# A seventh head pair's scores from fp32 operands, the last output tile's last product in column halves, and a new set of planner constants

## The chip, the cores and the metric

The kernel runs on one core of a Trainium2 chip. The metric is the device time of one execution in microseconds. A profiled execution has a time of its own and, inside it, a span from the first to the last instruction; positions in the trace are counted from the start of the span. All times below are microseconds unless marked ns.

## The reference

Attention with a causal mask over 4 batches of 12 heads, 448 positions, 64 columns a head, and then a block on the joined heads (768 channels):

```python
scores = scale * np.matmul(q, k.transpose(0, 1, 3, 2))
scores = np.where(mask, -1000000000.0, scores)
attn = np.exp(scores - max) / (sum + 1e-09)
x = (attn @ v), heads joined to (4, 448, 768)
theta = x @ w_theta
y = einsum(w_tok_r, x * cos(theta)) + einsum(w_tok_i, x * sin(theta))
u = x + y
out = u + np.maximum(u @ w_ch, 0.0)
```

Inputs and outputs are fp32; the weights arrive as fp64 and are brought to fp32 on the chip.

## The kernel before

**Numbers in two parts.** Most matmul operands are split into a rounded part and a remainder (both F32R tiles), and a product is made from two or three of the combinations. A product of two unsplit fp32 operands is written as one matmul, which the trace shows as two instructions.

**Attention.** Heads go in pairs, six pairs to a batch, 24 in all. `load_pair` brings a pair's q, k and v. A pair whose number is under `KN["NQ"]` (6) takes the fp32 way: k into one `kk` buffer (ring of 3) and each head's half of q into the two zero-padded `qz` tiles, slot `pr % 2`, three loads in all. Every later pair takes the split way: k and q into `kr` and `qr` (one buffer each), a rounding copy and a subtraction for each (L402, L403, recorded at L331 to L342), and then four stores from SBUF to SBUF for each head (L409, L411), which lay the two parts into `kk` and `qs`. `head` makes the four score blocks of a head, 448, 336, 224 and 112 columns wide: L441 by fp32, L444 by two F32R matmuls. VectorE masks and finds the minimum (L447), ScalarE makes the exponential and its sums (L450), TensorE transposes (L474), ScalarE or VectorE copies the result back (L334, L336). A pair's sums are turned into reciprocals (L457, L458), transposed (L459, in the one-bank PSUM ring `xo`), copied (L460), stored to DRAM (`rd<-rs`) and read back spread over the partitions (`rb<-rd`, one buffer). The product with v (L491) uses the same `xo` bank, which L494 frees as it multiplies it by `rb` into `xT`.

**The block on the heads.** `weight` decodes w_theta and w_tok; `batch` makes theta (L540), sine and cosine, and the mix over positions (L620). `project` makes the last product for batches 1 and 2 (L682). `pair` makes it for batches 3 and 0 together by seven smaller products of three 128-row output tiles each (L749). `block` prepares the three operand chunks `ub` of each such product: a rounding copy and a subtraction. `last` finishes an output tile: an addition of the bank to a partial sum (`add`, recorded at L757), a maximum with zero and an addition (L769), and the store. The last of the seven products (`s4`, with `end`) goes tile by tile, so that the last tile's nine matmuls stand alone at the end.

**The order.** No order is written out. Every operation gets a due time `P.now`, and `Plan.order` lays all of them out by a list schedule: at each moment a free engine takes the ready operation with the smallest due time, an engine that is not the first choice counting `AP` or `AQ` later. The resulting sequence is the program order of each engine and of the queue on SyncE (SP), which issues every DMA. The constants in `KN` set the due times: `S0`, `P0`, `P1` the pace of the heads (`tau`); `TL`, `RL`, `V`, `BB` the transposes, reciprocals and products with v; `LD`, `SL`, `SH` the loads and splits of q and k; `LW`, `W0`, `WT`, `W1`, `WK`, `E0`, `CR` the weights; `M0`, `MR`, `MR2`, `X0`, `XL`, `EX` a batch's block; `O0`, `OR` the last products; `UL`, `UD` the chunks `ub`, of which chunk c is due at the clock of the products less `UL` plus `UD` times c; `SB`, `SC` the combined weights. Up to due time `AE` GpSimd may take copies.

Of the kernel before, what the change touches and what calls it, by code (L numbers as in the profile page):

```python
# [13 lines left out]
ALU = mybir.AluOpType  # L14
# [4 lines left out]
MAGIC = 12582912.0  # L19


KN = dict(S0=-2520.8995, P0=3914.469, P1=7056.6972, V=0.0339, TL=0.8835, RL=-0.0438, SL=7631.8556, SH=2896.8187,
          LD=2238.5021, LW=-1908.5532, M0=-3353.0467, MR=1.7842, MR2=-0.0229, W0=15032.9046, WT=3030.4005,
          W1=2485.321, WK=2746.2629, E0=-8178.3792, CR=419.9564, O0=2180.1597, OR=0.4535, X0=-265.4206, NS=1, PR=2,
          AE=15377.7073, BB=-1728.1953, AP=5033.1175, AQ=2425.1203, XT=3, NQ=6, WP=2, NW=4, EX=0.4254, PORT=1,
          DW=1450, DE=150, DB=250.0, SL2=0, UL=1823.0792, UD=372.3266, SB=51637.6906, SC=462.9947, XL=-895.2931,
          TS=0.2508, SW=3360.6242, WQ=2)


class Buf:  # L30
# [11 lines left out]
class Plan:  # L42
# [12 lines left out]
    def op(self, eng, dur=None, fn=None, r=(), w=(), lat=None, pr=None, table=None, after=(), port=("POOL",), pen="AP", mode="m"):  # L55
        o = Op()
        o.pen = KN[pen]
        o.port = port
# [38 lines left out]
    def order(self):  # L97
# [53 lines left out]
        while done < len(self.ops):  # L151
# [10 lines left out]
            for e in free:  # L162
# [3 lines left out]
                for o in ready[e]:  # L166
                    if port > t and e in o.port and KN["PORT"]:
                        continue
                    if best is not None and (o.pr > best.pr + KN["SW"] or turn(last[0], o.mode)):
                        continue  # L170
# [23 lines left out]
                if o.wire:  # L194
                    wire = max(wire, fin + KN["DW"]) + o.wire
                    end = wire + KN["DE"]
                out.append((t, o.idx, o))
# [10 lines left out]
                for x in o.succ:  # L208
                    x.n -= 1
                    x.ready = max(x.ready, end + max(delay(e, a) for a in x.alts) + KN["SL2"])  # L210
                    if not x.n:
# [8 lines left out]
def attention_moe_kernel(  # L220
# [10 lines left out]
    nc = tc.nc  # L231
    B, NP, _, S = q.shape
# [27 lines left out]
    P = Plan(rings)  # L260
# [35 lines left out]
    def pe(n, m=128):  # L296
        return {112: 75, 224: 102.5, 336: 153, 384: 173.7, 448: 206.7}[n]

    def dv(n):
        return n / 0.96 + 68  # L300
# [13 lines left out]
    def dma(fns, nbytes, r=(), w=(), pr=None, after=(), half=False):  # L314
        def run():
            for f in fns():
                nc.sync.dma_start(out=f[0], in_=f[1])  # L317
        n = nbytes[0]
        o = P.op("SP", 530 if n == 1 else 615.0 * n, run, r, w, lat=0, pr=pr, after=after)
        o.wire = nbytes[1] / KN["DB"]  # L320
        return o
# [3 lines left out]
    def copy(n, o, i, r, w, psum=False, engs=("DVE", "ACT"), after=()):  # L325
        alts = []
        if not psum and P.now <= KN["AE"]:
            engs = tuple(engs) + ("POOL",)
# [10 lines left out]
    def alu(n, o, a, b, op, r, w, engs=("POOL", "DVE"), after=(), pool=False):  # L339
        if P.now > KN["AE"] and not pool:  # L340
            engs = ("DVE",)
# [6 lines left out]
    def boost(h):  # L348
        return KN["BB"] * max(0, h % H - (H - 3)) / 2
# [33 lines left out]
    def load_pair(pr):  # L383
        b, p = divmod(pr, NP)
        t0 = tau(2 * pr)
        if pr < KN["NQ"]:
            kp = buf("kk", [128, 2, S])
            dma(lambda: [(kp.t[:, 0], k[b, p])], (1, 229376), [], [kp], pr=t0 - KN["LD"] - 50000)
            for hh in range(2):
                own = slice(64 * hh, 64 * hh + 64)  # L390
                qz, i = QZ[hh], pr % 2
                dma(lambda qz=qz, own=own, i=i: [(qz.t[own, i], q[b, p, own])], (1, 114688), [], [(qz, i)],
                    pr=t0 - KN["LD"] + hh - 49999)
                KS[2 * pr + hh], QS[2 * pr + hh] = kp, (qz, i)
        else:
            t1 = t0 - KN["SL"]
            parts = []
            for n, (ring, src) in enumerate((("kr", k), ("qr", q))):
                y = buf(ring, [128, 2, S], F32R)
                dma(lambda y=y, src=src: [(y.t[:, 1].bitcast(F32), src[b, p])], (1, 229376), [], [(y, 0), (y, 1)], pr=t1 - KN["LD"])  # L400
                P.now = t1 + 300 * n
# [12 lines left out]
        vs = buf("vs", [TQ, NJ, 2, D])  # L414
        dma(lambda: [(vs.t, v[b, p])], (1, 229376), [], [vs], pr=t0 - KN["LD"] + 1000)
        VS[pr] = vs
# [6 lines left out]
    def head(h):  # L423
# [42 lines left out]
        for n, js in enumerate(((2,), (3, 1), (0,))):  # L466
            P.now = t0 + per * (KN["TL"] + (1.5, 3, 4)[n] * KN["TS"]) - boost(h)
            pt = buf("t", [TQ, S])
# [190 lines left out]
        return clock[0]  # L659

    NC = KD // 2


    def project(b, wb, t0, rate, after):
# [10 lines left out]
        for m in range(KD):  # L675
            cp = buf("st"[m % 2], [128, 512], F32, "cp")
            for p in range(KD):
                wt, wk = wb[2 * (m // NC) + p // NC]

                def mm(p=p, m=m, cp=cp, wt=wt):  # L680
                    for n, (w2, a) in enumerate(((0, 0), (0, 1), (1, 0))):
                        nc.tensor.matmul(out=cp.t[:, 0:S], lhsT=wt()[:, p % NC, w2, 128 * (m % NC):128 * (m % NC) + 128],  # L682
                                         rhs=us[p].t[:, a], start=(p == 0 and n == 0), stop=(p == KD - 1 and n == 2))
# [11 lines left out]
    def pair(ba, bb, xa, xb, t0, rate, wb, ws, after, end=False):  # L695
        clock = [t0]
        ka = lambda p: [(xa, (p, 0)), (xa, (p, 1))]
        kb = lambda p: [(xb, (p, 0)), (xb, (p, 1))]
        ua = lambda p: (lambda: xa.t[:, p])
        vb = lambda p: (lambda: xb.t[:, p])  # L700
        u2, u3 = buf("R", [128, NC, S], F32, "u2"), buf("R", [128, NC, S], F32, "u3")
        q1 = buf("xs", [128, NC, S], F32, "q1")

# [37 lines left out]
        def product(w, ub, banks, first, inner=True):  # L741
            wt, wk = w
            for x in range(NC):
                for y in range(NC):
                    m, c = (y, x) if inner else (x, y)

                    def mm(m=m, c=c):
                        for n, (w2, a) in enumerate(((0, 0), (0, 1), (1, 0))):
                            nc.tensor.matmul(out=banks[m].t[:, 0:S], lhsT=wt()[:, c, w2, 128 * m:128 * m + 128],  # L749
                                             rhs=ub[c].t[:, a], start=(first and c == 0 and n == 0),  # L750
                                             stop=(c == NC - 1 and n == 2), skip_group_check=True)
                    clock[0] += 3 * pe(S) * rate
                    P.now = clock[0]
                    P.op("PE", 3 * pe(S), mm, [(ub[c], 0), (ub[c], 1)] + wk(c), [banks[m]])

        def add(o, a, b, op, r, w):
            P.op("DVE", dv(S), lambda: nc.vector.tensor_tensor(out=o(), in0=a(), in1=b(), op=op), r, w)  # L757
# [5 lines left out]
                port=("POOL",) if rd and rd[0] is not ot else ("POOL", "DVE"))  # L763
            dma(lambda: [(out[b, 128 * n:128 * n + 128, :], ot.t)], (1, 229376), [ot], [])

        def last(z, uu, m, n):
            o = lambda: uu.t[:, m]
            add(o, lambda: z.t[:, 0:S], o, ALU.add, [z], [(uu, m)])
            P.op("DVE", dv(S), lambda: nc.vector.scalar_tensor_tensor(  # L769
                out=o(), in0=o(), scalar=0.0, in1=vb(n)(), op0=ALU.max, op1=ALU.add), kb(n), [(uu, m)], port=("POOL", "DVE"))  # L770
            dma(lambda: [(out[bb, 128 * n:128 * n + 128, :], o())], (1, 229376), [(uu, m)], [])

        def bank(ring):
            return buf(ring, [128, 512], F32, "cp")
# [24 lines left out]
        Z = [bank("m"), bank("t"), bank("m")]  # L799
# [2 lines left out]
            last(Z[m], u3, m, NC + m)  # L802
        product(s4, block(plain(vb, NC)), Z, False, not end)
        for m in range(NC):
            last(Z[m], u2, m, m)
        return clock[0]


# [26 lines left out]
    for i in range(NTK):  # L835
        weight(w_tok[i], S, wtk, i, bwtk, tau(H) + KN["W1"] + KN["WK"] * i, KN["WP"])
    n_att = len(P.ops)
    w_ops = [o for o in P.ops if "SP" not in o.alts]
    for b in range(B):
# [4 lines left out]
        if b == B - 1:  # L844
# [10 lines left out]
            for c in range(NC):  # L855
                for i, (n, p, hf) in enumerate(((0, c, 0), (1, NC + c, 0), (2, c, 1), (3, NC + c, 1))):
                    tt = tau(NH + 2) + KN["E0"] + KN["CR"] * (4 * c + i)
                    c0 = HW * hf
                    raw, z = buf("zh", [128, 2 * HW], I32, "rawc"), buf("zl", [128, 2, HW], F32, "zc")
# [118 lines left out]
```

## Time and profile before

| | |
|---|---|
| median of 3 runs | 484.84 (483.5 to 486.14) |
| the profiled execution | 482.89 |
| its span | 481.1 |
| TensorE (PE) busy | 467.7 |
| weight loads (PEld) busy | 397.7 |
| VectorE (DVE) busy | 396.6 |
| ScalarE (ACT) busy | 281.9 |
| GpSimd (POOL) busy | 17.6 |
| bytes moved by DMA | 68.34 MB |
| mean granted TensorE clock | 0.998 of full speed |

A row of a timeline gives start, duration, engine, line, operation, output and inputs, and in brackets the engine's idle time before it with what ended it. Matmuls are pipelined: a new one starts before the one ahead of it has ended, so the distance between starts is what one costs, not its duration. The table by stretches gives the busy time of each engine between two positions.

### The profile page before, as it was taken

Reading aid. Unit: us, or ns where it says so; the run is one execution under the profiler, and the core shown is the slowest. Engines: PE = TensorE matmul, PEld = TensorE weight load, DVE = VectorE, ACT = ScalarE, POOL = GpSimd, SP = SyncE. Lnnn points to the kernel's source line nnn. Section 1 sums busy time; section 2 is a strip of 40 time slices with the busy share of each in tenths; the row PEclk is TensorE's granted clock in tenths of the full one; section 3 lists DMA queues with packets and bytes.
Section 4 is the critical chain, followed back from the end, with each engine's and each line's share of the span. In section 5 each row is a group of like instructions: output and inputs, shape, how many; then the busy total and the mean of one; then the engine's idle time right before and its main releaser. Section 6 shows DMA issues by size and latency. Waiting matters only on the chain.

```text
span 481.1 us, 8541 instructions
## 1 busy us (share of the span) xinstructions
PE 467.7 (97%) x2813; PEld 397.7 (83%) x2813; DVE 396.6 (82%) x1092; ACT 281.9 (59%) x697; POOL 17.6 (4%) x21
## 2 busy tenths in 40 slices
PE   8989899999999999999999999999999999999996
PEld 4655676898887988898888988889798999999995
DVE  4998999879988676898966689984699999968766
ACT  4878689679855455998644659962546722403110
POOL 1202011000000000000000000000000000000000
PEclk9999999999999999999999999999999999999999
DMA  7876787566767576645666664501155200241113
GB/s 240 272 239 192 227 212 201 167 182 172 195 175 199 159 187 164 155 116 154 169 178 143 147 151 136 136 20 53 38 159 148 75 0 20 77 153 38 59 39 134
DMA packets 34651, 68.34 MB, mean 142 GB/s; under 512 B 5680, under 2 KB 24112, under 8 KB 34608
## 3 DMA queue, kind: packets, MB, share of 16 engines
q1 hardware_dynamic: 34608, 67.81, 50.7%
q8 instruction: 22, 0.36, 0.3%
q14 instruction: 21, 0.17, 0.1%
HBM read 36.04 MB, written 6.97 MB: 89 GB/s over the span
## 4 chain that ended last, share of the span: by engine, by line
PE 78%; DVE 11%; DMA 8%; SPq 2%; issue 1%; DVEq 0%
PE y L620 20%; PE th L540 15%; PE cp L682 8%; PE cp L749 8%; PE xo L491 7%; PE t L474 7%; PE s L444 7%; DMA rb<-rd 6%; PE s L441 2%; DVE e L447 2%; SPq L317 2%; PE xp L600 2%; DMA rd<-rs 1%; DVE xT L494 1%; DVE xs L523 1%
## 5 line engine op out<-in xcount | busy, mean ns | idle before, releaser
L450 ACT ACTIVATE e<-e,sm 112x448 f32<-112x448 f32 x192 | 100.5, 524 | 49.1 <-DVE sm L447 47.8
L540 PE MATMUL th<-wth,xs 128*128 128x384 f32 x528 | 111.2, 345 | 1.2 <-DVE R L562 1.1
L447 DVE CUSTOM_DVE_ANT_0 e<-s,mask 112x448 f32<-112x448 f32 x192 | 82.8, 440 | 25.2 <-PE s L444 18.5
L620 PE MATMUL y<-wtk,zh 128*128 128x448 f32 x336 | 98.7, 375 | 0.0
L540 PEld LDWEIGHTS th<-wth,xs 128*128 128x128 f32 x528 | 90.3, 188 | 6.2 <-issue 1.6
L474 PE MATMUL t<-ident,e 112*112 112x112 f32 x480 | 61.9, 260 | 1.9 <-ACT p L334 1.9
L444 PE MATMUL s<-kk,qs 128*112 128x448 f32 (+3 forms) x288 | 63.3, 306 | 0.2
L620 PEld LDWEIGHTS y<-wtk,zh 128*128 128x128 f32 x336 | 58.7, 189 | 3.8
L620 PE MATMUL y<-wtk,zl 128*128 128x448 f32 x168 | 61.3, 365 | 0.0
L474 PEld LDWEIGHTS t<-ident,e 112*112 112x112 f32 x480 | 50.9, 133 | 9.9 <-ACT p L334 2.9
L491 PE MATMUL xo<-p,vs 112*64 112x448 f32 (+3 forms) x384 | 51.0, 406 | 0.0
L444 PEld LDWEIGHTS s<-kk,qs 128*112 128x112 f32 x288 | 47.2, 175 | 4.5 <-DVE sm L447 0.9
L682 PE MATMUL cp<-ub,wa 128*128 128x448 f32 x216 | 46.2, 369 | 0.0
L334 ACT COPY p<-t 112x448 f32<-112x448 f32 (+1 forms) x80 | 35.6, 456 | 15.9 <-PE t L474 15.7
L491 PEld LDWEIGHTS xo<-p,vs 112*64 112x64 f32 x384 | 25.3, 136 | 23.7 <-issue 11.3
L682 PEld LDWEIGHTS cp<-ub,wa 128*128 128x128 f32 x216 | 40.1, 188 | 4.2 <-DVE wa L342 0.6
L336 DVE COPY p<-t 112x448 f32<-112x448 f32 (+1 forms) x64 | 34.1, 542 | 5.0 <-PE t L474 4.8
L450 ACT ACTIVATION_READ_ACCUMULATOR e<-e,sm 112x1 f32 x192 | 36.0, 187 | 0.0
L620 PEld LDWEIGHTS y<-wtk,zl 128*128 128x128 f32 x168 | 31.5, 188 | 2.8
L441 PE MATMUL s<-kk,qz 128*112 128x448 f32 (+3 forms) x96 | 29.3, 419 | 2.1 <-DVE sm L447 1.2
L494 DVE TENSOR_TENSOR xT<-xo,rb 128x448 f32<-128x448 f32 x24 | 14.9, 622 | 18.6 <-PE xo L491 11.1
L441 PEld LDWEIGHTS s<-kk,qz 128*112 128x112 f32 x96 | 14.2, 178 | 10.7 <-DVE sm L447 4.7
(105 smaller groups left out, 616.5 us busy)
## 6 DMA issues: line engine op xcount, KB each, us to landing
kk<-kr SPq DMA_DIRECT2D x72, 224.0 KB
qs<-qr SPq DMA_DIRECT2D x72, 112.0 KB
vs<-v SPq DMA_DIRECT2D x24, 224.0 KB
rb<-rd SPq DMA_DIRECT2D x48, 112.0 KB
raw<-w_theta SPq DMA_DIRECT2D x6, 768.0 KB
rawc<-w_ch SPq DMA_DIRECT2D x12, 384.0 KB
kr<-k SPq DMA_DIRECT2D x18, 224.0 KB
qr<-q SPq DMA_DIRECT2D x18, 224.0 KB
```

Of the source, the lines that this page charges most:

```text
L334: alts.append((e, ac(n, 0 if psum else 1), lambda: nc.scalar.copy(out=o(), in_=i())))
L336: alts.append((e, dv(n) if psum else dv2(n), lambda: nc.vector.tensor_copy(out=o(), in_=i())))
L441: nc.tensor.matmul(out=s.t[:, 0:w], lhsT=qs[0].t[:, qs[1], TQ * j:TQ * j + TQ], rhs=kk.t[:, 0, 0:w])
L444: nc.tensor.matmul(out=s.t[:, 0:w], lhsT=qs.t[:, TQ * j:TQ * j + TQ], rhs=kk.t[:, t, 0:w], start=(t == 0), stop=(t == 1))
L447: P.op("DVE", dv(w) + 8, lambda j=j, w=w, s=s, e=e: nc.vector.tensor_tensor_reduce(out=e.t, in0=s.t[:, 0:w], in1=mask[:, S - w:S], scale=- ...
L450: P.op("ACT", ac(w, 2.5), lambda j=j, e=e: nc.scalar.activation(out=e.t, in_=e.t, func=AF.Exp, scale=-1.0, bias=sm.t[:, 0, hh, j:j + 1], a ...
L474: nc.tensor.transpose(pt.t[:, TQ * n:TQ * n + TQ], E[i].t[:, TQ * j:TQ * j + TQ], ident[0:TQ, 0:TQ])
L491: nc.tensor.matmul(out=xo.t[64 * a:64 * a + 64, TQ * j:S], lhsT=vs.t[:, j, a], rhs=pt(h - 1 + a, j), start=(j == 0), stop=(j == NJ - 1))
L540: nc.tensor.matmul(out=th.t[:, 0:HW], lhsT=l, rhs=wth[:, p, w2, c0:c0 + HW], start=(p == 0 and n == 0), stop=(p == KD - 1 and n == len(ops ...
L620: nc.tensor.matmul(out=y.t[:, 0:S], lhsT=l.t[:, c], rhs=wtk[:, c, w2], start=(c == 0 and n == 0), stop=(c == NTK - 1 and n == 2))
L682: nc.tensor.matmul(out=cp.t[:, 0:S], lhsT=wt()[:, p % NC, w2, 128 * (m % NC):128 * (m % NC) + 128], rhs=us[p].t[:, a], start=(p == 0 and n ...
L749: nc.tensor.matmul(out=banks[m].t[:, 0:S], lhsT=wt()[:, c, w2, 128 * m:128 * m + 128], rhs=ub[c].t[:, a], start=(first and c == 0 and n == 0),
```

## The change

`NQ` goes from 6 to 7, so the first pair of batch 1 (pair 6, heads 12 and 13) takes the fp32 way. The nine matmuls of the last output tile become eighteen of half the columns, all chunks of the first half ahead of those of the second, in the same PSUM bank; that tile's addition, its second VectorE pass and its store become two each. All planner constants except `NS`, `PR`, `XT`, `WP`, `NW`, `PORT`, `DW`, `DE`, `DB`, `SL2` and `WQ` have new values.

```diff
-KN = dict(S0=-2520.8995, P0=3914.469, P1=7056.6972, V=0.0339, TL=0.8835, RL=-0.0438, SL=7631.8556, SH=2896.8187,
-          LD=2238.5021, LW=-1908.5532, M0=-3353.0467, MR=1.7842, MR2=-0.0229, W0=15032.9046, WT=3030.4005,
-          W1=2485.321, WK=2746.2629, E0=-8178.3792, CR=419.9564, O0=2180.1597, OR=0.4535, X0=-265.4206, NS=1, PR=2,
-          AE=15377.7073, BB=-1728.1953, AP=5033.1175, AQ=2425.1203, XT=3, NQ=6, WP=2, NW=4, EX=0.4254, PORT=1,
-          DW=1450, DE=150, DB=250.0, SL2=0, UL=1823.0792, UD=372.3266, SB=51637.6906, SC=462.9947, XL=-895.2931,
-          TS=0.2508, SW=3360.6242, WQ=2)
+KN = dict(S0=-2322.2295, P0=3825.9683, P1=7049.4592, V=-0.1301, TL=0.9548, RL=-0.0126, SL=7193.5981, SH=2093.2489,
+          LD=-533.577, LW=-2204.82, M0=-3622.2824, MR=1.7844, MR2=-0.0337, W0=14441.4741, WT=3425.2134, W1=1596.4928,
+          WK=2001.1803, E0=-6015.5099, CR=152.2681, O0=3470.174, OR=0.2314, X0=-990.0797, NS=1, PR=2, AE=6714.7344,
+          BB=-1147.7937, AP=5199.2148, AQ=3034.4501, XT=3, NQ=7, WP=2, NW=4, EX=-0.0, PORT=1, DW=1450, DE=150,
+          DB=250.0, SL2=0, UL=2542.8881, UD=2828.253, SB=239565.2892, SC=460.4297, XL=-486.3376, TS=0.2481,
+          SW=3382.3259, WQ=2)
...
+            for z in range(0 if inner else 2):
+                for c in range(NC):
+                    def mm(c=c, z=z):
+                        for n, (w2, a) in enumerate(((0, 0), (0, 1), (1, 0))):
+                            nc.tensor.matmul(out=banks[NC - 1].t[:, H2 * z:H2 * z + H2], lhsT=wt()[:, c, w2, 128 * NC - 128:128 * NC],
+                                             rhs=ub[c].t[:, a, H2 * z:H2 * z + H2], start=False,
+                                             stop=(c == NC - 1 and n == 2), skip_group_check=True)
...
-        def last(z, uu, m, n):
+        def last(z, uu, m, n, parts=1):
+            w = S // parts
+            for i in range(parts):
+                q = slice(w * i, w * i + w)
...
+                P.op("DVE", dv(w), lambda q=q, o=o: nc.vector.tensor_tensor(
+                    out=o(), in0=z.t[:, q], in1=o(), op=ALU.add), rd, to)
+                P.op("DVE", dv(w), lambda q=q, o=o: nc.vector.scalar_tensor_tensor(
+                    out=o(), in0=o(), scalar=0.0, in1=vb(n)()[:, q], op0=ALU.max, op1=ALU.add), kb(n) + to, to, port=("POOL", "DVE"))
+                dma(lambda q=q, o=o: [(out[bb, 128 * n:128 * n + 128, q], o())], (1, 229376 // parts), to, [])
...
-            last(Z[m], u2, m, m)
+            last(Z[m], u2, m, m, 2 if end and m == NC - 1 else 1)
```

## Rows read from the trace of the kernel before

**Rows 1.** Busy time by stretch: length, then PE, PEld, DVE, ACT, POOL, clock, DMA

```profile
12.00:36.00 24.00, 22.61 (x136) 14.61 (x135) 23.72 (x78) 18.96 (x55) 3.94 (x3) 1.00 0.80 255
36.00:60.00 24.00, 21.49 (x129) 14.32 (x128) 21.84 (x75) 17.56 (x53) 3.77 (x3) 1.00 0.73 210
60.00:96.00 36.00, 34.27 (x230) 26.27 (x230) 32.84 (x110) 28.82 (x86) 4.18 (x3) 1.00 0.72 193
96.00:336.00 240.00, 239.51 (x1583) 211.29 (x1580) 193.80 (x581) 163.73 (x409) 0.00 (x0) 1.00 0.58 150
336.00:348.00 12.00, 10.90 (x63) 9.01 (x62) 7.10 (x17) 5.74 (x12) 0.00 (x0) 1.00 0.11 29
348.00:468.00 120.00, 119.87 (x606) 109.65 (x605) 104.01 (x197) 41.46 (x69) 3.46 (x3) 1.00 0.24 77
```

**Rows 2.** PE's waits from 12 to 96: total, times, longest

```profile
PE t L474 <- ACT p L334: 1.9, 3, 1.2
PE xo L459 <- DVE xT L494: 1.8, 3, 1.2
PE s L441 <- DVE sm L447: 0.7, 1, 0.7
```

**Rows 3.** The chain that ended last, 40 to 58: start, duration, what

```profile
40.84 0.59 SPq L317
...
42.12 6.14 DMA rb<-rd
...
53.52 4.29 DMA rb<-rd
```

**Rows 4.** DMA issues: engine, operation, count, size of each

```profile
kk<-kr SPq DMA_DIRECT2D x72, 224.0 KB
qs<-qr SPq DMA_DIRECT2D x72, 112.0 KB
```

**Rows 5.** Timeline of VectorE: the remainder of q for pair 6

```profile
41.74 0.56 DVE L342 TENSOR_TENSOR qr<-qr 128x448 fp32r<-128x448 f32 x1
```

**Rows 6.** Timeline of PE: one head's fp32 scores (L441), and split scores (L444)

```profile
54.75 1.57 PE L441 MATMUL s<-kk,qz 128*112 128x448 f32 x4
56.16 0.74 PE L474 MATMUL t<-ident,e 112*112 112x112 f32 x6
56.74 0.74 PE L441 MATMUL s<-kk,qz 128*112 128x224 f32 x4
57.33 0.28 PE L474 MATMUL t<-ident,e 112*112 112x112 f32 x1
...
88.59 0.88 PE L444 MATMUL s<-kk,qs 128*112 128x448 f32 x4
89.31 0.69 PE L540 MATMUL th<-wth,xs 128*128 128x384 f32 x3
...
91.27 0.52 PE L444 MATMUL s<-kk,qs 128*112 128x224 f32 x4
91.62 0.57 PE L540 MATMUL th<-wth,xs 128*128 128x384 f32 x2
```

**Rows 7.** Timeline of the last 17 us: operand chunks, last products, last passes

```profile
465.38 11.32 PE L749 MATMUL cp<-ub,wth 128*128 128x448 f32 x54
...
466.82 0.62 DVE L342 TENSOR_TENSOR ub<-xT,ub 128x448 fp32r<-128x448 f32 x1
...
476.73 0.62 DVE L757 TENSOR_TENSOR u<-cp,u 128x448 f32<-128x448 f32 x1 [0.57 <-PE cp L749]
477.39 0.62 DVE L769 SCALAR_TENSOR_TENSOR u<-u,xT 128x448 f32<-128x448 f32 x1
```

**Rows 8.** Groups by line and shape: VectorE copies out of PSUM, full and half width

```profile
L336 DVE COPY p<-t 112x448 f32<-112x448 f32 x44 | 27.0, 616 | 4.1 <-PE t L474 4.0
L336 DVE COPY p<-t 112x224 f32<-112x224 f32 x20 | 7.6, 380 | 0.8 <-PE t L474 0.8
```

**Rows 9.** DMA in the last stretch that moved bytes, columns as in the first group

```profile
479.00:480.00 1.00, 0.00 (x0) 0.00 (x0) 0.00 (x0) 0.00 (x0) 0.00 (x0) 0.73 0.51 190
```

More of the change, by code (lines that the diff above doesn't have):

```diff
@@ L661, in attention_moe_kernel @@
     NC = KD // 2
+    H2 = S // 2
     def project(b, wb, t0, rate, after):
@@ L745, in product @@
                     m, c = (y, x) if inner else (x, y)
+                    if m == NC - 1 and not inner:
+                        break
                     def mm(m=m, c=c):
@@ L754, in product @@
                     P.op("PE", 3 * pe(S), mm, [(ub[c], 0), (ub[c], 1)] + wk(c), [banks[m]])
+            for z in range(0 if inner else 2):
[5 more added lines that the diff above has]
+                                             stop=(c == NC - 1 and n == 2), skip_group_check=True)
+                    clock[0] += 330 * rate
+                    P.now = clock[0]
+                    P.op("PE", 330, mm, [(ub[c], 0), (ub[c], 1)] + wk(c), [(banks[NC - 1], z)])
         def add(o, a, b, op, r, w):
@@ L764, in emit @@
             dma(lambda: [(out[b, 128 * n:128 * n + 128, :], ot.t)], (1, 229376), [ot], [])
-        def last(z, uu, m, n):
[L767 to L771, printed above, removed]
+        def last(z, uu, m, n, parts=1):
+            w = S // parts
+            for i in range(parts):
+                q = slice(w * i, w * i + w)
+                o = lambda q=q: uu.t[:, m, q]
+                rd = [z] if parts == 1 else [(z, i), (uu, m)]
+                to = [(uu, m if parts == 1 else (m, i))]
+                P.op("DVE", dv(w), lambda q=q, o=o: nc.vector.tensor_tensor(
[3 more added lines that the diff above has]
+                dma(lambda q=q, o=o: [(out[bb, 128 * n:128 * n + 128, q], o())], (1, 229376 // parts), to, [])
         def bank(ring):
```

## The prediction

> **What bounds the kernel now.** I read the busy time by stretch first [rows 1]. From 96 to 336 TensorE is busy 239.51 of 240 us, and from 348 to 468 119.87 of 120: no wait is left there, and only less work on TensorE, or a denser order of it, would shorten these stretches. Up to 96 it is otherwise. TensorE stands idle 24 - 22.61 = 1.39 us from 12 to 36, 24 - 21.49 = 2.51 from 36 to 60 and 36 - 34.27 = 1.73 from 60 to 96, 5.63 in all, while VectorE is busy 23.72, 21.84 and 32.84 us of the same stretches. From 336 to 348 another 12 - 10.90 = 1.10 us are idle. So the time is TensorE's work plus its idle time, and the change is worth the idle time it takes out less the work it adds.
>
> TensorE's waits up to 96 say what holds it [rows 2]: 1.9 us for ScalarE's copies of the transposed blocks, 1.8 us for L494 (the `xo` bank), 0.7 us for VectorE's minimum. The chain of waits shows what is behind L494 [rows 3]: the readback `rb<-rd`, 6.14 us in one pair and 4.29 us in the next. The next pair's reciprocals need the bank that L494 frees, so a slow readback holds the whole chain of pairs.
>
> **Pair 6 by fp32: what it removes.** Between the two readbacks lie the SBUF to SBUF stores of pair 6. A split pair makes 72 / 18 = 4 stores of 224 KB and 4 of 112 KB [rows 4], 1,344 KB. The fp32 way has none; its k and q loads carry the same 448 KB as before, in three issues instead of two. So ten issues become three on SP's queue. At about 0.59 us an issue [rows 3] that is some 4 us of SP time, which the `rd` and `rb` transfers queued behind them no longer see. Two remainders on VectorE go too, near 0.56 us each [rows 5], 1.1 us of an almost full engine, with two rounding copies that lay on ScalarE.
>
> Worth on the path: if the 6.14 us readback comes down to the next one's 4.29, it gains 1.85 us, which covers the longest L494 wait, 1.2 us [rows 2, 3]. The 0.7 us for the minimum stands behind these remainders on VectorE; I count it as gone. Of ScalarE's 1.9 us I count half, 0.9. That is 1.2 + 0.7 + 0.9 = 2.8 us recovered. The bounds are 0 (VectorE and SP are filled at once by weight decoding moved earlier) and the whole 5.63 us. I take the middle, because the first two waits have the removed work right ahead of them and the rest has not.
>
> **What it adds.** For a head, distances between starts give the fp32 cost [rows 6]: 56.16 - 54.75 = 1.41 us for the 448 and 336 wide blocks and 57.33 - 56.74 = 0.59 for the other two, against 89.31 - 88.59 = 0.72 and 91.62 - 91.27 = 0.35 by the split way. That is 0.93 us more a head and **1.9 us** a pair. It falls at about 65 to 80, where idle time could cover some of it; once the idle time is counted as recovered above, it is paid in full. The two `qz` slots and the `kk` ring have one more user each: a load of pair 6 waits at the head of SP's queue until pair 4's scores release its slot. Behind it are weight loads and readbacks; VectorE would be late next. I leave it at 0 (cover: the loads are due far ahead; at worst one wait of the size of the 1.2 us one [rows 2]).
>
> **The last tile.** The last product's last tile is nine matmuls, each 11.32 / 54 = 0.210 us [rows 7], so it starts near 476.73 - 1.89 = 474.84. Its passes of 0.62 us follow one after the other to 478.01. A half-width pass is about 0.38: copies from PSUM took 616 ns and 380 ns [rows 8]. In halves TensorE needs between 0 and 0.2 us more, by the 0.35 us that two 224 and two 112 wide matmuls took [rows 6]. If VectorE may work on the first half while TensorE writes the second, only 2 x 0.38 us remain behind the last matmul instead of 2 x 0.62: 0.3 to 0.5 us sooner. If the two engines may not be in the bank together, the planner's order decides. By the code's durations the first half's addition is laid after two of the second half's three chunks, because the tile before it still has VectorE. The third chunk then waits for a 0.38 us pass, and the end is 474.84 + 0.95 (nine half matmuls) + 0.65 (six) + 0.38 + 0.33 (three) + 0.80 (two half passes) = 477.95 and the hand-overs between the engines, as late as before. The smaller last store gains at most half of 0.51 us [rows 9]. So between 0.75 us sooner and 0.2 later (the addition behind all matmuls); I take **0.2 sooner**, since both halves lie in one bank.
>
> On this the Trainium skill speaks against the change: its page "PSUM — Partial Sum Buffer", section "PSUM bank collisions raise a hardware error", says that TensorE writing and VectorE reading one bank and 32-partition quadrant at once is an error, at disjoint columns too, so that the two must be kept apart by bank and not by address. No row here shows two engines in one bank. By that rule the halves cannot overlap and the term is 0.2; without it, 0.6.
>
> **The constants.** Their effect lies in the order only. `P1` moves by 0.1% and `MR` not at all, so the long full stretches should keep their pattern; a denser or looser order of transposes, scores and long products there is worth something I can't read from rows, so I put it at 0 with 1.1 us, the one visible gap, to either side. Moving `O0` from 2180 to 3470 and `M0` from -3353 to -3622 makes the chunks `ub` due 1.6 us later against batch 3's own splits. In the gap at 336 to 348 ScalarE and VectorE work on both, so I count half of the 1.10 us as recovered [rows 1], between -0.5 and 1.1. `SB` leaves the combined weights behind everything else, as before. `AE` takes one copy of w_theta from GpSimd: 0.
>
> **Sum.** 1.9 - 2.8 - 0.2 - 0.55 = -1.6 us (rounded). The profiled execution (482.89, of which the span is 481.1) is 1.95 us under the median of the runs, so I apply the change to the median: 484.84 - 1.6 = **483.2**.
>
> **The rivals.** *The chain of pairs comes free:* with less traffic every readback gets shorter, and nearly all idle time before 96 goes (4.8 of 5.63), with the whole gap at 336 and the tail's overlap: 1.9 - 4.8 - 1.1 - 0.6 = -4.6, 480.2. For it speaks that three of the four waits hang on VectorE or on a readback; against it, that weight decoding (`W1`, `WK`) moves into the same place.
>
> *Nothing is recovered:* decoding fills what pair 6 leaves and the fp32 passes are paid in full: 1.9 - 0.2 = +1.7, 486.5. VectorE's 23.72 of 24 us before 36 speaks for it.
>
> *Late operand chunks in the last products (slower):* `UL` and `UD` make the third chunk due 4.19 us later against its product's clock (from -1.08 to +3.11). In before, the last product's third remainder ended at 467.44 and was first needed six matmuls into it, at 465.38 + 27 x 0.21 + 6 x 0.21 = 472.3 [rows 7], so 4.9 us of cover. If two 0.62 us passes get ahead of it after the cover is used up, a product waits 1.24 us; from four of the seven products on it decides: 4 x 1.24 - 1.6 = +3.3, 488.1. Against it: VectorE is busy only 104 of 120 us there [rows 1], and a due time only orders what is ready.
>
> *It doesn't do what it says* holds for the tail alone (no overlap in one bank), and is inside the forecast.
>
> **How the numbers follow.** The forecast has 0.45, with its own range 481.2 to 485.3; about a quarter of it lies under the bound for faster. The free chain has 0.27, nothing recovered 0.13, late chunks 0.15. A measurement of this kernel can tell about 0.5%, 2.4 us, from no change. Faster by more: 0.27 + 0.10 = 0.37. Within: 0.35 + 0.13 = 0.48. Slower: 0.15. The range that leaves out the far ends of the first and last rival is 479.7 to 487.2.
>
> **What would show it.** Right: L441 has 112 instructions and `kk<-kr` 68 or fewer; the readback near 42 falls to about 4.3; PE's idle time from 12 to 96 falls from 5.6 to near 3; the fp32 scores run to about 72; the gap near 346 is half as long or gone; the end after the last matmul is 0.2 to 0.5 us shorter. Wrong: PE busy from 348 to 468 falls below 119 of 120 (late chunks), or the idle time before 96 stays above 5 (nothing recovered), or the sum of PE busy changes by over 1 us beyond the added 1.9, which would be the order and not the edit.

## The result, and the profile after

| | before | after |
|---|---|---|
| median | 484.96 (483.5 to 486.14, 4 runs) | 478.95 (478.58 to 479.47, 4 runs) |
| ratio of the medians, 95% interval | | 0.9878 (0.9849 to 0.9907) |
| the profiled execution, its span | 482.89, 481.1 | 478.76, 477.0 |
| TensorE busy | 467.65 | 468.16 |
| TensorE idle, 12 to 96 | 5.63 | 1.96 |

The change makes the kernel faster by 6.0 us, 1.2%. The two profiled executions are only 4.1 us apart, because that of before lies some 2 us under its median; a second profile of before, below, shows what can lie between its executions. The stretches of after, with the columns of [rows 1]:

```profile
12.00:36.00 24.00, 23.79 (x147) 15.89 (x145) 23.49 (x78) 20.12 (x60) 3.89 (x2) 1.00 0.79 247
36.00:60.00 24.00, 23.10 (x138) 15.47 (x138) 23.73 (x82) 19.50 (x57) 3.23 (x2) 1.00 0.71 211
60.00:96.00 36.00, 35.15 (x236) 27.00 (x233) 31.87 (x109) 26.25 (x81) 0.00 (x0) 1.00 0.66 184
96.00:336.00 240.00, 239.87 (x1585) 210.56 (x1584) 198.67 (x596) 163.82 (x406) 0.00 (x0) 1.00 0.57 147
336.00:348.00 12.00, 12.00 (x68) 11.69 (x67) 9.20 (x22) 2.73 (x5) 0.00 (x0) 1.00 0.32 83
348.00:468.00 120.00, 119.11 (x596) 108.41 (x595) 103.67 (x192) 38.22 (x64) 3.45 (x3) 1.00 0.23 73
```

The second number of a row is TensorE's busy time. What it lacks to the length is idle time, against [rows 1]: 5.63 to 1.96 us from 12 to 96 (-3.67), 1.10 to 0 from 336 to 348, 0.49 to 0.13 from 96 to 336, but 0.13 to 0.89 from 348 to 468. With 0.11 more ahead of 12 and 0.35 less from 468 to the end, the idle time fell by 4.61 us while busy time rose by 0.51: -4.1, the distance of the two profiles. So the time came out of waits, four fifths of it ahead of 96. The gap at 336 did not simply close. It was a wait for VectorE's L562, and after has a shorter wait for L562 further on; every profile here has one of the two and none has both. Timelines of TensorE in before and in after:

```profile
346.86 2.37 PE L540 MATMUL th<-wth,xs 128*128 128x384 f32 x12 [1.09 <-DVE R L562]
```

```profile
364.87 0.55 PE L600 MATMUL xp<-ident,xT 128*128 128x128 f32 x3 [0.74 <-DVE R L562]
```

From 336 to 468 the idle time goes from 1.10 + 0.13 = 1.23 to 0.89 us, 0.34 less.

TensorE's waits in after, 12 to 110, as in [rows 2] (total, times, longest), and then VectorE's wait for the readback from 12 to 96, first in before and then in after:

```profile
PE t L474 <- ACT p L334: 0.9, 1, 0.9
PE s L444 <- DVE sm L447: 0.6, 2, 0.4
PE xo L459 <- DVE xT L494: 0.2, 1, 0.2
```

```profile
DVE xT L494 <- DMA rb<-rd: 4.3, 4, 1.9
```

```profile
DVE xT L494 <- DMA rb<-rd: 0.6, 1, 0.6
```

The wait for L494 that [rows 2] show with 1.8 us is down to 0.2, and VectorE, which had stood still for 4.3 us behind late readbacks, stands still for 0.6.

### The profile page after: what moved, and what is told of

It is laid out like the page before. It is cut to its first block, busy times and chain, and to the rows that moved or that the text cites. A ratio compares the mean times of both kernels' runs of the same rounds, so it can differ in the third digit from the quotient of the medians.

```text
span 477.0 us, 8550 instructions
## 1 busy us (share of the span) xinstructions
PE 468.2 (98%) x2822; PEld 398.1 (83%) x2822; DVE 401.3 (84%) x1109; ACT 276.0 (58%) x682; POOL 12.8 (3%) x17
## 4 chain that ended last, share of the span: by engine, by line
PE 84%; DVE 9%; DMA 4%; issue 1%; ACT 1%; SPq 0%; DVEq 0%; ACTq 0%
PE y L620 21%; PE th L540 17%; PE xo L491 9%; PE cp L683 9%; PE cp L753 8%; PE t L474 8%; PE s L444 7%; PE s L441 4%; DVE e L447 2%; DMA rb<-rd 1%; PE xp L600 1%; DMA kr<-k 1%; DMA kk<-kr 1%; DVE zw L360 1%; DVE p L336 1%
## 5 line engine op out<-in xcount | busy, mean ns | idle before, releaser
L447 DVE CUSTOM_DVE_ANT_0 e<-s,mask 112x448 f32<-112x448 f32 x192 | 83.1, 440 | 17.7 <-PE s L444 9.3
L474 PE MATMUL t<-ident,e 112*112 112x112 f32 x480 | 63.2, 260 | 0.9 <-ACT p L334 0.9
L444 PE MATMUL s<-kk,qs 128*112 128x448 f32 (+3 forms) x272 | 59.1, 301 | 0.6 <-DVE sm L447 0.6
L491 PE MATMUL xo<-p,vs 112*64 112x448 f32 (+3 forms) x384 | 51.0, 406 | 0.0
L444 PEld LDWEIGHTS s<-kk,qs 128*112 128x112 f32 x272 | 45.6, 175 | 4.0 <-DVE sm L447 0.9
L491 PEld LDWEIGHTS xo<-p,vs 112*64 112x64 f32 x384 | 25.3, 136 | 24.7 <-issue 13.2
L441 PE MATMUL s<-kk,qz 128*112 128x448 f32 (+3 forms) x112 | 35.4, 421 | 1.3 <-DVE sm L447 0.4
L334 ACT CAST zh<-C 128x512 fp32r<-128x512 f32 x19 | 11.8, 619 | 25.6 <-DVE C L603 20.8
L441 PEld LDWEIGHTS s<-kk,qz 128*112 128x112 f32 x112 | 16.2, 178 | 10.7 <-DVE sm L447 5.4
```

What stands on the lines that cost most here:

```text
L334: alts.append((e, ac(n, 0 if psum else 1), lambda: nc.scalar.copy(out=o(), in_=i())))
L441: nc.tensor.matmul(out=s.t[:, 0:w], lhsT=qs[0].t[:, qs[1], TQ * j:TQ * j + TQ], rhs=kk.t[:, 0, 0:w])
L444: nc.tensor.matmul(out=s.t[:, 0:w], lhsT=qs.t[:, TQ * j:TQ * j + TQ], rhs=kk.t[:, t, 0:w], start=(t == 0), stop=(t == 1))
L447: P.op("DVE", dv(w) + 8, lambda j=j, w=w, s=s, e=e: nc.vector.tensor_tensor_reduce(out=e.t, in0=s.t[:, 0:w], in1=mask[:, S - w:S], scale=- ...
L474: nc.tensor.transpose(pt.t[:, TQ * n:TQ * n + TQ], E[i].t[:, TQ * j:TQ * j + TQ], ident[0:TQ, 0:TQ])
L491: nc.tensor.matmul(out=xo.t[64 * a:64 * a + 64, TQ * j:S], lhsT=vs.t[:, j, a], rhs=pt(h - 1 + a, j), start=(j == 0), stop=(j == NJ - 1))
```

## The experiments

Each ratio is to runs of the kernel before on the same chip, with its 95% interval. "Idle time" is TensorE's from 12 to 96 in the profile.

**The two halves of the change apart.** The kernel before with a seventh fp32 pair and nothing else:

```diff
-XT=3, NQ=6, WP=2
+XT=3, NQ=7, WP=2
```

> The kernel before with NQ=7 alone: old constants, last tile whole. Theory T (traffic): pair 6's eight SBUF to SBUF stores and its splitting were what held the pairs, so this alone recovers most of the 3.7 us of TensorE idle time between 12 and 96 and lands 2 to 4 us under before. Theory C (constants): the new due times recover it, and NQ alone only adds fp32 passes: 0 to 2 us over before, with 5 us or more of idle time still there.

482.33, ratio 0.9953 (0.9927 to 0.9979). Idle time 4.14 us; the gap at 336 to 348 stands at its 1.10. The time is what theory T said, but less than half of the 3.67 us of idle time comes back. What does come back lies at the readback: VectorE waits 1.4 us for it instead of 4.3, and the one that took 6.14 us [rows 3] takes 4.99 here, in the chain of this run:

```profile
41.34 4.99 DMA rb<-rd
```

The changed kernel with the old count:

```diff
-XT=3, NQ=7, WP=2
+XT=3, NQ=6, WP=2
```

> The changed kernel with NQ back at 6: new constants and halves, pair 6 by the split way. Theory T: the idle time before 96 comes back (5 us or more) and the kernel is 3 to 5 us over the changed one. Theory C: it keeps the short idle time and is within 2 us of the changed one, perhaps under it by up to 1.9 us of fp32 passes.

488.46, ratio 1.007 (1.0038 to 1.0101). Idle time 6.45 us. So there are four corners: 484.8 (old constants, six pairs), 482.3 (old, seven), 488.5 (new, six), 478.95 (new, seven); the two new ones have the halves too, which e3 below finds worth nothing. The new constants cost 3.6 us with six fp32 pairs and gain 3.4 with seven; the seventh pair gains 2.5 with the old constants and 9.5 with the new. Neither part has a price of its own. Waits of e2's VectorE, 12 to 96 (this file's lines are 5 lower, L355 is L360 of after), and two stretches of it:

```profile
DVE zw L355 <- DMA raw<-w_tok: 3.7, 1, 3.7
```

```profile
60.00:96.00 36.00, 30.71 (x178) 23.15 (x177) 27.32 (x89) 22.76 (x68) 1.14 (x1) 0.91 0.69 196
...
72.00:76.00 4.00, 4.00 (x19) 3.22 (x19) 2.38 (x10) 1.42 (x5) 0.00 (x0) 0.65 0.88 225
```

It is a late weight load that VectorE waits for here, not a readback, and the granted clock is 0.65 in a stretch that follows.

**The tail.** The changed kernel with its last tile whole:

```diff
-            last(Z[m], u2, m, m, 2 if end and m == NC - 1 else 1)
+            last(Z[m], u2, m, m)
```

(and the loop over halves taken out of `product`)

> The changed kernel with the last tile whole. Both theories: the end after the last matmul is as in before, and the time is 0.2 to 0.5 us over the changed kernel, too little for the rounds to tell; the trace's last stretch decides.

478.76, ratio 0.9882 (0.9832 to 0.9931): the halves are worth nothing that can be measured. The next kernel gives the second half a PSUM bank of its own:

```diff
+        Z3 = bank("s") if end else None
-        product(s1, block(mixed(B1, A1 + sub)), Z, True)
+        product(s1, block(mixed(B1, A1 + sub)), Z, True, z3=Z3)
...
-    nc.tensor.matmul(out=banks[NC - 1].t[:, H2 * z:H2 * z + H2], ...
+    nc.tensor.matmul(out=(banks[NC - 1], z3)[z].t[:, H2 * z:H2 * z + H2], ...
```

> The changed kernel with the second half of the last tile in a PSUM bank of its own, in the product before it too. If the two engines had to keep out of one bank, the third chunk of the second half no longer waits for the first half's addition (0.48 us of TensorE idle time there is gone) and the distance from the start of the tile's matmuls to the end falls by 0.4 to 0.7 us. If the wait had another cause, the distance stays. The whole time moves by under 1 us, too little for the rounds.

478.43, ratio 0.9873 (0.9843 to 0.9904): against after no difference that can be told. The trace shows one. Timeline of the tail, first after, then this kernel:

```profile
470.72 0.62 DVE L787 TENSOR_TENSOR u<-cp,u 128x448 f32<-128x448 f32 x1
...
472.39 0.39 DVE L787 TENSOR_TENSOR u<-cp,u 128x224 f32<-128x224 f32 x1 [0.38 <-PE cp L763]
472.82 0.39 DVE L789 SCALAR_TENSOR_TENSOR u<-u,xT 128x224 f32<-128x224 f32 x1
472.84 0.59 PE L763 MATMUL cp<-ub,wth 128*128 128x224 f32 x3 [0.48 <-DVE u L787]
473.47 0.39 DVE L787 TENSOR_TENSOR u<-cp,u 128x224 f32<-128x224 f32 x1 [0.26 <-PE cp L763]
473.89 0.39 DVE L789 SCALAR_TENSOR_TENSOR u<-u,xT 128x224 f32<-128x224 f32 x1
```

```profile
471.03 2.16 PE L776 MATMUL cp<-ub,wth 128*128 128x224 f32 x18
471.24 0.62 DVE L801 TENSOR_TENSOR u<-cp,u 128x448 f32<-128x448 f32 x1
472.44 0.38 DVE L801 TENSOR_TENSOR u<-cp,u 128x224 f32<-128x224 f32 x1
472.85 0.39 DVE L803 SCALAR_TENSOR_TENSOR u<-u,xT 128x224 f32<-128x224 f32 x1
473.23 0.39 DVE L801 TENSOR_TENSOR u<-cp,u 128x224 f32<-128x224 f32 x1
473.65 0.39 DVE L803 SCALAR_TENSOR_TENSOR u<-u,xT 128x224 f32<-128x224 f32 x1
```

In one bank the third chunk of the second half stands 0.48 us behind the first half's addition; in two the eighteen matmuls run through. From the start of the tile-before's addition to the end of the span it is 6.23 us in before (474.87 to 481.1), 6.16 in e3, 477.0 - 470.72 = 6.28 in after and 476.7 - 471.24 = 5.46 in two banks. Against the whole tile (6.23 and 6.16) the split gains 0.7 to 0.8 us in two banks and nothing in one, in these single profiles.

**Which constants.** The changed kernel with the constants of the blocks and last products as before:

```diff
-M0=-3622.2824, MR=1.7844, MR2=-0.0337, E0=-6015.5099, CR=152.2681, O0=3470.174, OR=0.2314,
-X0=-990.0797, UL=2542.8881, UD=2828.253, SB=239565.2892, SC=460.4297, XL=-486.3376
+M0=-3353.0467, MR=1.7842, MR2=-0.0229, E0=-8178.3792, CR=419.9564, O0=2180.1597, OR=0.4535,
+X0=-265.4206, UL=1823.0792, UD=372.3266, SB=51637.6906, SC=462.9947, XL=-895.2931
```

> The changed kernel with the thirteen constants of the block on the heads and the last products (M0, MR, MR2, E0, CR, O0, OR, X0, UL, UD, SB, SC, XL) as before. If these closed the gap at 336 to 348, the gap of about 1 us comes back and the time rises by 1 to 1.5 us; if the front alone made the gain, the time stays within 0.7 us of the changed kernel.

480.68, ratio 0.991 (0.987 to 0.9949). Idle time 2.98 us. Its stretch at the gap:

```profile
336.00:348.00 12.00, 12.00 (x68) 11.72 (x67) 9.96 (x23) 3.50 (x7) 0.00 (x0) 1.00 0.24 68
```

With the old `O0` and `M0` this stretch stays full, and the wait for L562 (0.74 us) stands at 366.7 as in after: what I took the gap to hang on is not what moves it. Then seven fp32 pairs and the halves on the old constants, with only the loads' and weights' group new, and with only the attention's group new:

```diff
-SL=7631.8556, SH=2896.8187, LD=2238.5021, LW=-1908.5532, W0=15032.9046, WT=3030.4005, W1=2485.321, WK=2746.2629
+SL=7193.5981, SH=2093.2489, LD=-533.577, LW=-2204.82, W0=14441.4741, WT=3425.2134, W1=1596.4928, WK=2001.1803
```

> The changed kernel with NQ=7 and halves, but of the constants only the eight of loads and decoding new (W0, WT, W1, WK, LW, LD, SL, SH), the rest as before. The old constants with NQ=7 gave 482.3, all new ones 478.9. Theory W: when loads and decoding are issued decides, so this lands within 1 us of 478.9, with under 3 us of TensorE idle time from 12 to 96. Theory A (the due times of the attention decide): it stays within 1 us of 482.3 with 4 us of idle time.

```diff
-S0=-2520.8995, P0=3914.469, P1=7056.6972, V=0.0339, TL=0.8835, RL=-0.0438, TS=0.2508, BB=-1728.1953,
-AP=5033.1175, AQ=2425.1203, AE=15377.7073, SW=3360.6242, EX=0.4254
+S0=-2322.2295, P0=3825.9683, P1=7049.4592, V=-0.1301, TL=0.9548, RL=-0.0126, TS=0.2481, BB=-1147.7937,
+AP=5199.2148, AQ=3034.4501, AE=6714.7344, SW=3382.3259, EX=-0.0
```

> As the run before it, but with the attention's constants new (S0, P0, P1, V, TL, RL, TS, BB, AP, AQ, AE, SW, EX) and those of loads and decoding as before. Theory A: within 1 us of 478.9, idle time from 12 to 96 under 3 us, and the gap of 1.1 us at 336 to 348 gone. Theory W: within 1 us of 482.3, with 4 us of idle time.

483.23, ratio 0.9972 (0.9945 to 0.9999), and 483.81, ratio 0.999 (0.9962 to 1.0019). Neither group alone does better than e1 with neither. Idle time is 4.08 and 3.80, near e1's 4.14. The gap at 336 to 348 is there in e8 (1.09) and gone in e9, which has the shorter wait at 368.4 in its place, so the attention's group moves it. Only both groups together (e4) come under the 482.3 of e1, by 1.7 us in the medians; the third set brings another 1.7. The intervals of e4 overlap with those of e1 and of after, so these two steps are not clear of noise.

**What the seventh pair takes away.** I tried to put pair 6's split work back as dummies, unread, into the changed kernel: its k and q loads, splits and eight stores (e5), the same without the splits (e6), with the stores cut to 32 columns (e11), with the stores into buffers of their own in DRAM (e12).

```diff
-        else:
+        if pr >= KN["NQ"] or pr == 6:
...
+                if pr < KN["NQ"]:        # e6, e11, e12: no rounding, no remainder
+                    parts.append(y)
+                    continue
```

> The changed kernel, in which pair 6's loads into kr and qr, its splitting and its eight SBUF to SBUF stores are made as before but nobody reads them; the scores stay fp32. Theory T (the removed preparation made the gain): 8 us or more over the changed kernel, as the run with NQ=6 and new constants, plus the fp32 passes. Theory P (only the order of scores and loads counts): within 2 us of the changed kernel.

488.62, ratio 1.0079 (1.0048 to 1.011), idle time 5.07.

> As the run before it, but without the splitting on VectorE, ScalarE and GpSimd: only the two loads and eight stores of pair 6 are left, which nobody reads. If the bytes and SP's issues are what held the pairs, it is as slow as the run with the whole preparation (within 1.5 us). If the four split operations on the filled engines were, it is within 2 us of the changed kernel.

493.63, ratio 1.0186 (1.0148 to 1.0224), idle time 9.74.

> The run with pair 6's loads and stores alone (493.6), in the same order on every engine and queue and into the same buffers, but each of the eight stores carries 32 columns of one part instead of all (kk 8 KB instead of 224, qs 8 instead of 112). Theory B (bytes on the DMA engines): without them most of the 15 us goes, and it lands under 484. Theory Q (SP's queue: the ten issues, their wait for a kk or qs buffer, and the order the planner made around them): it stays within 3 us of 493.6.

493.84, ratio 1.0165 (1.0121 to 1.0209), idle time 9.77.

> The same loads and eight stores with all their bytes, but into DRAM buffers of their own, so that they neither wait for nor take a kk or qs buffer. Theory B: still 488 or more. If taking the three kk buffers was the matter (the split pairs' stores and the fp32 loads behind them in SP's queue wait for one), it lands within 3 us of the changed kernel, 478.9.

494.88, ratio 1.0203 (1.0167 to 1.0238), idle time 10.96. Less work gave a longer time (e6 over e5), and cutting the stores' bytes did nothing (e11). But the planner gave every engine another sequence in these four, so they price that sequence as well as the stores. They rule out the bytes, and the `kk` and `qs` buffers, as the whole cause of their own loss, and no more. e6 came as neither of its theories said.

So the last pair of kernels keeps after's sequence on every engine and only adds eight stores to SP's queue: two ahead of the fourth readback, four behind the next load of v, two ahead of the fifth readback. In e13 they carry pair 6's 1,344 KB, in e14 they are cut to 16 columns. The expectation takes these for the places of pair 6's stores, but they are one readback later. The trace of before has two of pair 6's at 40.29, ahead of the third readback (41.52), four at 43.90 and two at 50.82, ahead of the fourth (52.90). The added ones stand at 49.77, 53.20 and 63.44 in e14, among the stores of pair 7. So the two kernels price eight stores added there, and not pair 6's own in their place.

```diff
             if o.eng == "SP":
+                if any(b.ring == "rb" for b in o.bufs):
+                    seen["rb"] += 1
+                    if seen["rb"] in (4, 5):
+                        extra(2, 2)
+                elif seen["rb"] == 4 and not seen["qs"] and any(b.ring == "vs" for b in o.bufs):
+                    seen["qs"] = 1
+                    o.run()
+                    extra(4, 1)
+                    continue
```

> The changed kernel in its own order on every engine, with eight stores added to SP's queue at the places where pair 6's stood in before (two ahead of the fourth readback, four behind the next load of v, two ahead of the fifth readback), as large as those (four of 224 KB, four of 112 KB), from a constant tile into DRAM buffers that nobody reads. Theory B (bytes and SP issues cost by themselves): 2 us or more over the changed kernel (478.9), with TensorE idle between 36 and 60. Theory O (the stores cost through the order that the planner lays around them): within 1 us of it.

484.59, ratio 1.0007 (0.9983 to 1.0031), idle time 3.33.

> The same eight added stores with 16 columns instead of 448: issues without bytes. If issues cost, it is as slow as the run with the bytes; if bytes cost, it is within 0.5 us of the changed kernel; under theory O both are.

482.92, ratio 0.9951 (0.9925 to 0.9977), idle time 3.28. Eight issues with next to no bytes cost 0.0073 x 484.8 = 3.5 us over after (whose interval ends at 0.9907); the bytes cost another 1.7 us by the medians of this pair, 2.7 by the ratios, whose intervals just don't touch. The two profiles (spans of 481.7 and 482.0) don't show the bytes' part. The idle time that e13 was to have between 36 and 60 isn't there either (0.90 us, as in after); it lies behind 60. How issues cost, the timelines tell: first SP's queue and VectorE in after, then SP, VectorE and TensorE in e14.

```profile
47.78 0.29 SPq L317 DMA_DIRECT2D rd<-rs  x1
...
54.12 0.58 SPq L317 DMA_DIRECT2D raw<-w_tok  x1
```

```profile
60.12 0.72 DVE L360 TENSOR_SCALAR zw<-raw 128x448 uint16<-128x448 uint16 x2
```

```profile
49.42 0.30 SPq L317 DMA_DIRECT2D rd<-rs  x1
49.77 1.22 SPq L952 DMA_DIRECT2D ex<-mask  x2
...
53.20 2.39 SPq L952 DMA_DIRECT2D ex<-mask  x4
...
58.17 0.54 SPq L317 DMA_DIRECT2D raw<-w_tok  x1
```

```profile
64.50 0.72 DVE L360 TENSOR_SCALAR zw<-raw 128x448 uint16<-128x448 uint16 x2 [2.26 <-DMA raw<-w_tok]
```

```profile
65.44 0.82 PE L441 MATMUL s<-kk,qz 128*112 128x336 f32 x2 [0.79 <-DVE sm L447]
```

And e14 by stretches, right there:

```profile
64.00:68.00 4.00, 2.75 (x14) 1.44 (x13) 3.46 (x12) 2.54 (x7) 0.00 (x0) 0.99 0.64 199
68.00:72.00 4.00, 4.00 (x18) 2.79 (x18) 3.15 (x12) 3.21 (x12) 0.00 (x0) 0.59 0.98 282
```

Ahead of the stores e14 already runs 1.64 us late (49.42 against 47.78), by its first scores and not by the edit; more of that below. The weight load is issued 4.05 us later, so 2.41 us are the stores', as much as the four ahead of it keep the queue (2.39). The decoding step that needs it stands at the head of VectorE's sequence, so the score pass L447 behind it waits although its own input is there. Its result frees a score bank for TensorE, which stands still for 1.25 of these 4 us (0.79 in this one wait), and in the next 4 us TensorE runs at a granted clock of 0.59. Of the 5.0 us between the spans of e14 and after the late start takes 1.6; of the 3.4 that are left, 1.3 are idle time and some 1.6 (0.41 of 4 us, an estimate) the clock.

**The other end of the trade.** The changed kernel with an eighth fp32 pair:

```diff
-XT=3, NQ=7, WP=2
+XT=3, NQ=8, WP=2
```

> The changed kernel with NQ=8, so that pair 7's stores go too. If bytes and issues still bind, another 1 to 2 us come off. If little idle time is left to recover (about 2 us before 96 in the changed kernel), the 1.9 us of fp32 passes are paid nearly in full and it is 0.5 to 2 us slower than the changed kernel.

481.18, ratio 0.9932 (0.9909 to 0.9956), 2.2 us over after. Idle time is 1.59 against after's 1.96: there is hardly any left to take out. Its profile starts late too, by 1.75 us, so of the 3.4 us between the two spans 1.7 are left, near the 1.9 of the fp32 passes.

**The clock behind a wait.** A second profile of the kernel before:

> The kernel before, unchanged: a second profile. The listed runs of before spread from 481.7 to 488.1, and those with a lower mean granted clock are the longer ones. Theory K (clock): an execution with more idle time before 96 loses the full TensorE clock for some us there, which is where its profile would show it. If this execution has a mean clock under 0.998, the stretch with the lower clock lies between 24 and 96 and right behind idle time of TensorE; if its clock is 1.0, idle time before 96 is between 4 and 6 us as in the first profile.

486.22 against the first profile's 482.89, from the same sequence of instructions. Timeline of TensorE at the same place, in the first and in the second:

```profile
27.41 0.40 PE L474 MATMUL t<-ident,e 112*112 112x112 f32 x2 [1.21 <-ACT p L334]
27.95 1.01 PE L441 MATMUL s<-kk,qz 128*112 128x448 f32 x2
28.89 0.97 PE L491 MATMUL xo<-p,vs 112*64 112x448 f32 x4
```

```profile
29.19 0.40 PE L474 MATMUL t<-ident,e 112*112 112x112 f32 x2 [1.21 <-ACT p L334]
29.73 1.30 PE L441 MATMUL s<-kk,qz 128*112 128x448 f32 x2
30.96 1.76 PE L491 MATMUL xo<-p,vs 112*64 112x448 f32 x4
```

```profile
28.00:30.00 2.00, 0.77 (x4) 0.54 (x5) 2.00 (x9) 1.99 (x8) 0.00 (x0) 1.00 0.79 272
30.00:32.00 2.00, 2.00 (x6) 0.30 (x4) 2.00 (x10) 1.15 (x6) 0.00 (x0) 0.58 0.17 56
32.00:34.00 2.00, 2.00 (x7) 1.35 (x6) 2.00 (x4) 1.37 (x3) 0.00 (x0) 0.57 0.93 258
```

The last fence is the second profile by stretches. Both executions have the same 1.21 us of idle time. Behind it the granted clock stays at 1.00 in the first and is 0.58 and 0.57 in the second, so for most of those 4 us at the lower level, 1.2 GHz. Four matmuls of L491 take 1.76 instead of 0.97 us, and from the first score matmul to the second group of L491 it is 5.17 us instead of 3.63: a wait of 1.21 us has cost 1.5 more. The other 1.8 of the 3.3 us are there ahead of the wait. They come from the first scores, here in the first and in the second profile:

```profile
4.54 1.77 PE L441 MATMUL s<-kk,qz 128*112 128x448 f32 x4 [0.18 <-DMA qz<-q]
...
9.46 0.63 PE L441 MATMUL s<-kk,qz 128*112 128x224 f32 x2 [0.16 <-DVE sm L447]
```

```profile
4.98 6.10 PE L441 MATMUL s<-kk,qz 128*112 128x448 f32 x12 [0.62 <-DMA qz<-q]
11.24 0.63 PE L441 MATMUL s<-kk,qz 128*112 128x224 f32 x2 [0.16 <-DVE sm L447]
```

They begin 0.44 us later, and then the same twelve matmuls run 6.10 us without a pause, where the first profile has 4.2 us of them and waits between; the same two matmuls follow 1.78 us later. The stretches show a clock of 1.00 there, but that is no reading: the trace of the second has no record of the clock before 9.8 us, that of the first none before 5.0.

Of the 77 runs of before beside these experiments, the 35 with a mean granted clock of at least 0.998 have a median of 483.7, the 42 below it 486.1. The four runs of after are all at 0.998 or more.

## Why the prediction was wrong

**The number.** 483.2 was forecast, from 479.7 to 487.2; it is 478.95, 0.8 us under the range. The rival *the chain of pairs comes free*, 480.2, came nearest, and it had 0.27. Its waits went its way, but not as far: -3.67 of its 4.8 us ahead of 96, -0.34 of its 1.10 from 336 on, none of the overlap in the tail. That its sum of -4.6 lies near the -4.1 of the profiles is in part luck, because busy time rose by 0.51 and not by 1.9.

**What held.** L441 has 112 instructions and `kk<-kr` 68 issues. Groups by line, of before and then of after (instructions, busy time, mean):

```profile
L444 PE MATMUL s<-kk,qs 128*112 128x448 f32 (+3 forms) x288 | 63.3, 306 | 0.2
...
L441 PE MATMUL s<-kk,qz 128*112 128x448 f32 (+3 forms) x96 | 29.3, 419 | 2.1 <-DVE sm L447 1.2 <-issue 0.3 <-DMA qz<-q 0.2
```

```profile
L444 PE MATMUL s<-kk,qs 128*112 128x448 f32 (+3 forms) x272 | 59.1, 301 | 0.6 <-DVE sm L447 0.6
...
L441 PE MATMUL s<-kk,qz 128*112 128x448 f32 (+3 forms) x112 | 35.4, 421 | 1.3 <-DVE sm L447 0.4 <-issue 0.3 <-DMA qz<-q 0.3
```

35.4 + 59.1 - 29.3 - 63.3 = 1.9 us: the term of the fp32 passes [rows 6]. TensorE's whole busy time rose by only 0.51, so the other instructions stand 1.4 us denser; which ones, these rows don't tell. By the sign that I had set for it, over 1 us beside the added 1.9, this is the order and not the edit. The fp32 scores end at 72 as said, and no readback of after up to 96 that the trace times took more than 4.2 us, against the 4.3 I had named. The eighth pair (e10) cost 2.2 us where hardly any idle time was left to set against it.

**The idle time ahead of 96.** Forecast 2.8 us recovered, to near 3; it is 3.67, to 1.96. The terms were right in kind: L494's wait fell from 1.8 to 0.2, the one for the minimum [rows 2] from 0.7 to nothing for L441 and 0.6 for L444, ScalarE's from 1.9 to 0.9. But the removal alone (e1) brings only 5.63 to 4.14, 1.49 of the 2.8 us. The rest needs the new constants.

**The first step that failed: the constants at 0 ± 1.1.** Beside the gap, I gave the order no worth because I could read none from rows of the full stretches, and sized the doubt by the one visible gap. Measured, the new constants are worth 3.4 us with seven pairs (482.3 to 478.95), and cost 3.6 with six (e2). In the profiles forecast and result are 2.45 us apart (-1.65 and -4.1): 1.4 by the denser busy time, 0.9 by the idle time ahead of 96 and 0.36 by that from 96 to 336, with small terms either way. My half of the gap, 0.55, was meant to come from `O0` and `M0`; 0.34 came, and e4 and e9 have it without them.

**The second: a wait priced at its own length.** The sum goes by the profiled execution, whose clock stood at 1.00 up to 468, and was then laid on the median. The second profile of before has 3.3 us more that no idle row from 12 to 96 shows: 1.5 behind a wait of 1.21, and 1.8 by slower first scores. So -4.1 in the profiles is -6.0 in the medians. How the 1.9 us between divide over the two is not shown. The 35 runs of before with the higher mean clock (483.7) stand 4.8 us over after, whose four runs are all on that side.

**The cause, half right.** I counted 4 us of SP time for ten issues that become three, and then valued only what the readback had to gain from it, with the traffic as the reason. The readback did gain (e1), though two of pair 6's eight stores stand ahead of both readbacks and not between them. e14 shows that eight issues can cost 3.5 us with next to no bytes, and e13 1.7 to 2.7 more with them, but one readback later than pair 6's stood. How the gain of the seventh pair divides between issues and bytes is therefore not shown. And the one who waits is not always the readback: in before it is the readback (4.3 us of VectorE's time), in e2 and e14 a load of w_tok, 3.7 and 2.26 us. In e14 that late load stops the decoding step at the head of VectorE's sequence, and the score pass behind it.

**The tail.** Forecast 0.2 sooner. With the halves the last pass ends 3.56 us after the tile-before's addition begins, without them 3.14 (e3), so 0.42 later; the smaller store then ends 0.30 sooner after it (2.72 against 3.02). The order was the one that I read from the code, the third chunk behind the 0.39 us pass. But what I added up to 3.11 us from the tile's start to its last pass took 3.76 (470.52 to 474.28): the first fifteen half matmuls 1.83 instead of 1.60, the last three 0.59 instead of 0.33, and 0.16 more around the passes, the hand-overs that I named and left without a price. The Trainium skill's page "PSUM — Partial Sum Buffer", section "PSUM bank collisions raise a hardware error", wants two engines kept apart by bank and 32-partition quadrant, not by address. After keeps them apart in time, and no run here puts both into one bank at once, so the rule itself is not tested. e7 is in line with it: apart by bank the two overlap, 0.8 us sooner than in after.

**The slower rivals.** *Late operand chunks* did not come: the idle time from 348 to 468 rose to 0.89 us, under the 1 us I had set as its sign, and 0.74 of it is the wait at 364.87 for L562, not of a product for its chunk.

*Nothing is recovered* falls with 3.67 us.

**What stays open.** Which constants of the two groups must go together; which instructions stand denser; what pair 6's stores cost in their own place; how much of the loss in e5, e6, e11 and e12 is the planner's other sequence; and what lets the clock fall behind a wait, or the first scores run slower, in one execution and not in another.

## What to carry to other kernels

Count issues on a shared queue, not only bytes, and ask of each load behind them which in-order engine has its user at the head and who stands behind that user. A set of planner constants has no worth apart from the work that it was found for: judge the two together, or run all four corners. Where TensorE waits a microsecond here and there, price a wait above its length if some executions show a lower granted clock right behind it, and split an output tile into halves only if each half has a bank.

## What the runs showed of the hardware

The same 1.21 us of idle time is followed by a full clock in one execution and by 0.58 and 0.57 in another of the same program. Eight stores of 16 columns cost 3.5 us; each kept SP's queue for some 0.6 us, and a load behind four of them was issued 2.4 us later. And the start varies: in some profiles (the second of before, e10, e13, e14) the first scores began at 4.98 to 5.40 instead of 4.54 and 4.64, ran slower, and what followed stood 1.6 to 1.8 us later throughout.
